# Seven block products for the gradient of w_down, interleaved with those of w_gate and w_up

## The chip, the cores and the metric

The kernel runs on one core of a Trainium2 chip. The metric is device time in microseconds (us) of one execution of the whole program; lower is better. "Before" is the kernel without the change, "after" the one with it.

## The reference

The program is the forward and backward pass of one transformer block in bf16: a pre-norm linear-attention layer, then a pre-norm SwiGLU feed-forward layer, with sequence length 2048, width D = 640 and hidden width F = 1728. It returns the block's output and the gradients of x, wqkv, wo, w_gate, w_up and w_down. What matters here is the feed-forward half, with n the normalised input of that layer:

```python
g = silu(n @ w_gate)          # n: 2048 x 640, w_gate and w_up: 640 x 1728
u = n @ w_up
out = (g * u) @ w_down        # w_down: 1728 x 640
# backward, with dy = grad_out (2048 x 640), m = g * u, dm = dy @ w_down.T:
# d_w_gate = n.T @ dg     (640 x 1728)
# d_w_up   = n.T @ du     (640 x 1728)
# d_w_down = m.T @ dy     (1728 x 640); the kernel forms its transpose, dy.T @ m (640 x 1728)
```

All three weight gradients are sums over the 2048 tokens, that is 16 token tiles of 128 rows.

## The kernel before, in words

**Groups.** The feed-forward backward pass runs in four groups of hidden columns, numbered 0 to 3, of width w = 448, 448, 448 and 384 (`GW`, `GO`). A group has two stages.

**Stage one, the SwiGLU loop.** For each pair of token tiles t, t+1 TensorE forms n @ w_gate (`pg`, L731) and n @ w_up (`pu`, L736), and in group 2 also dm (`pdm`, L417). ScalarE makes the sigmoids and bf16 copies (L752 to L758), and VectorE seven elementwise products and sums (L764), which leave m in the tile `m_s` [128, 16, 448] and the gradients dg and du side by side in `dd[0]` (token tiles 0 to 7) and `dd[1]` (tiles 8 to 15).

**Staging.** The next stage of the program needs dg and du transposed. So for each token tile SyncE's queue issues a transposing DMA of that tile's dg and du from `dd` into a small staging tile `stg` (L767), and then a store from there to the DRAM scratch `scr_dT` (L720). `stg` has three buffers, used in turn; a tile's transpose waits for the store of the tile three before it. GpSimd's queue stores `m_s` to `scr_m`, four token tiles at a time (L772).

**Stage two, the weight gradients** (`dw_group`; called "the gradient stage" below). TensorE forms the gradients of the group's columns. Rows of each 640-row gradient are five tiles of 128, i = 0 to 4. For d_w_gate and d_w_up, tiles 0 to 3 are formed by a Winograd form of Strassen's algorithm: the tokens are halved (k = 0, 1), the rows are halved (m = 0, 1, two tiles each, u = 0, 1), and the columns are the two halves dg | du of `dd`; seven block products (`prod`, L646, eight matmuls of w columns for each u) replace eight. VectorE makes the sums of operands: `S` and `S3` from n (`hn`), and `T1` to `T4` from `dd`, written over parts of `dd` and `m_s` (all L642). ScalarE copies partial results out of PSUM (L673, L685, L689, L698), VectorE adds them up into `dwev` tiles, and GpSimd's queue stores those (L652). Tile 4 of d_w_gate and d_w_up, and all five tiles of the transposed d_w_down, are plain accumulations over 16 token tiles by the helper `dw` (matmul L806, copy out of PSUM L808, store L810).

The orders of TensorE, VectorE and ScalarE in the gradient stage are the order in which the code is written (a manual schedule), and every engine works through its queue in order. PSUM is four buffers `mm` of two banks; `fpool` has six buffers for SwiGLU temporaries and results on their way out.

**Around it.** After a group's last staging store SyncE goes on with other loads and transposes (L258, L713, L190). In group 3 ScalarE's queue issues the load of the first transposed columns (`cols`, L157) ahead of its copies. After group 3 comes the input gradient (`ps_dhn`, L108).

Of the kernel before, what the change touches and what calls it, by code (L numbers as in the profile page):

```python
# [20 lines left out]
def kernel(  # L21
# [591 lines left out]
    zpad = wB.enter_context(tc.tile_pool(name="zpool", bufs=1)).tile([P, 4, 64], BF16, name="zpad")  # L613
    nc.gpsimd.memset(zpad[:], 0.0)

    with tc.manual_schedule(engines={EngineType.SP}):
# [10 lines left out]
        def dw_group(g, w, m_s, dd, dw, dwd_part, dgu_part):


# [14 lines left out]
            def prod(out, lhs, rhs, first):  # L644
                for t in range(8):
                    nc.tensor.matmul(out, lhsT=lhs[:, t, :], rhs=rhs[:, t, :], start=(first and t == 0),  # L646
                                     stop=(t == 7), skip_group_check=not first)

            def store(ev, n, m):
                for u in range(2):  # L650
                    i = 2 * m + u
                    nc.gpsimd.dma_start(out=(out_4, out_5)[n][i * P:(i + 1) * P, GO[g]:GO[g] + w], in_=ev[:, u, :w])  # L652

            U = range(2)
# [669 lines left out]
```

## Time and profile before

| | |
|---|---|
| median of 3 runs | 796.48 us (796.11 to 797.13) |
| profiled execution, first to last instruction | 794.5 us |
| matmul busy | 790.2 us, 99% of the span, 5315 matmuls |
| VectorE busy | 566.9 us, 71% |
| ScalarE busy | 288.1 us, 36% |
| GpSimd busy | 172.7 us, 22% |

Times in views of the trace are us from the start of the span. In the page and the views PE is TensorE's matmuls, PEld its weight loads, DVE VectorE, ACT ScalarE, POOL GpSimd and SP SyncE; "SPq" rows are instructions of SyncE that issue a DMA. L with a number is a line of the kernel. A row of the timeline has start, length, engine, line, operation, the tiles written and read, the shape, the count, and in brackets how long the engine had been idle before and what ended that. Matmuls overlap: the time of one row runs to the end of its last matmul, and the next row starts before that. The median lies 2.0 us above the span: what lies around the first and the last instruction.

### The profile page before, as it was taken

The page shows a single profiled execution, that of the slowest core. Times are in us where ns is not written, and L with a number is a line of the kernel's source. Part 1 is how long each engine was busy: PE and PEld are TensorE (multiplying, and loading weights), DVE is VectorE, ACT ScalarE, POOL GpSimd, SP SyncE. Part 2 cuts the span into 40 slices and gives each one's busy share as a digit, 9 for nine tenths or more (in the row PEclk, how much of TensorE's full clock was granted, in tenths as well). Part 3 has the DMA queues.
Part 4 walks back from the last instruction along what each step waited for, and adds up shares of the span by engine and source line. Part 5 has one row for each costly group of instructions (what it writes and reads, how often), then busy time and mean ns, then how long its engine had stood idle before and what let it go on. Part 6 is the DMA issues. An engine that isn't in the chain of part 4 may idle for free.

```text
span 794.5 us, 13629 instructions
## 1 busy us (share of the span) xinstructions
PE 790.2 (99%) x5315; PEld 506.5 (64%) x5315; DVE 566.9 (71%) x1015; ACT 288.1 (36%) x414; POOL 172.7 (22%) x305
## 2 busy tenths in 40 slices
PE   9999999999999999999999999999999999999998
PEld 7776566555555555555666777777777777777665
DVE  7989988894497648845975259998897366635773
ACT  6962532760283045402831123223313133324010
POOL 4600047411201110012042102111221121113230
PEclk9999999999999999999999999999999999999999
DMA  9799999999679877892798657976598959999992
GB/s 259 161 241 305 198 225 254 257 264 234 176 160 236 211 175 191 217 246 68 147 216 217 247 152 193 211 197 168 127 238 177 177 135 155 189 223 261 208 259 83
DMA packets 286705, 160.11 MB, mean 202 GB/s; under 512 B 241564, under 2 KB 275485, under 8 KB 286640
## 3 DMA queue, kind: packets, MB, share of 16 engines
q1 hardware_dynamic: 268912, 99.56, 61.7%
q0 software_dynamic: 14832, 54.36, 22.4%
q10 hardware_dynamic: 2896, 5.33, 2.0%
q8 instruction: 41, 0.67, 0.4%
q14 instruction: 24, 0.20, 0.1%
HBM read 47.68 MB, written 53.66 MB: 128 GB/s over the span
## 4 chain that ended last, share of the span: by engine, by line
PE 97%; DMA 1%; DVE 1%; POOL 0%; issue 0%; SPq 0%; DVEq 0%
PE ps_dhn L108 15%; PE ps_dw L806 10%; PE ps_dxn L1069 8%; PE pu L736 7%; PE ps_wa L646 7%; PE pg L731 7%; PE ps_dwqk L986 5%; PE ps_dm L417 5%; PE ps_kq L305 4%; PE ps_oa L1139 4%; PE ps_wc L646 3%; PE ps_gt L861 3%; PE ps_dp L108 3%; PE ps_dk L108 3%; PE ps_y L508 3%; PE ps_a L571 3%
## 5 line engine op out<-in xcount | busy, mean ns | idle before, releaser
L108 PE MATMUL ps_dhn<-wgT,cols 128*128 128x320 bf16 x864 | 119.5, 299 | 0.0
L108 PEld LDWEIGHTS <-cols 128*128 128x128 bf16 x864 | 84.5, 98 | 32.9
L146 DVE CUSTOM_DVE_ANT_0 lb_a<-lb_dy,hn 128x640 bf16<-128x640 bf16 x32 | 26.4, 825 | 59.0 <-ACT lb_dy L144 59.0
L736 PE MATMUL pu<-wgu,hnT 128*128 128x448 bf16 (+1 forms) x320 | 63.6, 346 | 0.0
L731 PE MATMUL pg<-wgu,hnT 128*128 128x448 bf16 (+1 forms) x320 | 63.6, 346 | 0.0
L806 PE MATMUL ps_dw<-m_s,dh 128*128 128x448 bf16 (+1 forms) x320 | 60.4, 346 | 0.0
L1069 PEld LDWEIGHTS <-ring 128*128 128x128 bf16 x480 | 47.0, 98 | 18.2
L1069 PE MATMUL ps_dxn<-wqkvT,ring 128*128 128x320 bf16 x320 | 51.3, 299 | 0.0
L736 PEld LDWEIGHTS <-hnT 128*128 128x128 bf16 x320 | 31.3, 98 | 27.1
L806 PEld LDWEIGHTS <-dh 128*128 128x128 bf16 x320 | 31.3, 98 | 27.1
L731 PEld LDWEIGHTS <-hnT 128*128 128x128 bf16 x320 | 31.3, 98 | 27.0
L417 PEld LDWEIGHTS <-dh2T 128*128 128x128 bf16 x320 | 31.0, 98 | 25.1
L417 PE MATMUL ps_dm<-wdT,dh2T 128*128 128x448 bf16 (+1 forms) x240 | 46.5, 344 | 0.0
L144 ACT ACTIVATE lb_dy<-ps_dhn,rstd 128x640 bf16<-128x640 f32 x16 | 12.7, 794 | 91.5 <-PE ps_dhn L108 91.5
L305 PE MATMUL ps_kq<-wqk,xnT 128*128 128x320 bf16 x320 | 44.9, 299 | 0.3 <-DMA wqk<-in_A_wqkv_dram 0.2
L752 ACT ACTIVATE dd<-pg 128x896 bf16<-128x896 f32 (+1 forms) x32 | 28.5, 891 | 40.4 <-PE pg L731 38.0
L642 DVE TENSOR_TENSOR dd<-dd 128x3584 bf16<-128x3584 bf16 (+1 forms) x12 | 23.1, 1954 | 22.8 <-PE ps_wa L646 15.6
L305 PEld LDWEIGHTS <-xnT 128*128 128x128 bf16 x320 | 30.9, 98 | 12.7 <-issue 0.5
L646 PEld LDWEIGHTS <-S 128*128 128x128 bf16 x256 | 25.1, 98 | 21.7
L772 POOL DMA_DIRECT2D scr_m<-m_s x16 | 12.1, 758 | 122.6 <-DVE m_s L764 122.6
L986 PEld LDWEIGHTS <-hn 128*128 128x128 bf16 x320 | 31.0, 98 | 12.0
L150 ACT ACTIVATE lb_a<-hn,lb_k 128x640 bf16<-128x640 bf16 x32 | 29.5, 920 | 21.8 <-DVE lb_k L149 18.8
(210 smaller groups left out, 1527.1 us busy)
## 6 DMA issues: line engine op xcount, KB each, us to landing
scr_dT<-stg SPq DMA_DIRECT2D x48, 224.0 KB, 2.6
cols<-scr_dT POOLq DMA_DIRECT2D x6, 1728.0 KB, 8.4
scr_m<-m_s POOLq DMA_DIRECT2D x12, 448.0 KB, 4.6
cols<-scr_dT ACTq DMA_DIRECT2D x2, 1728.0 KB, 10.5
scr_dT<-stg SPq DMA_DIRECT2D x16, 192.0 KB, 2.3
scr_pq<-pqa SPq DMA_DIRECT2D x4, 640.0 KB, 4.6
scr_xnT<-xnT SPq DMA_DIRECT2D x4, 640.0 KB, 5.3
scr_pk<-pk SPq DMA_DIRECT2D x4, 640.0 KB, 4.6
```

The lines of the kernel that those rows point to most:

```text
L108: nc.tensor.matmul(ps[:, ci, :320], lhsT=lhs(k), rhs=rhs(k, *NCH[ci]), start=(start and k == 0), stop=(stop and k == n - 1))
L150: nc.scalar.activation(out=a[:], in_=xhat, func=ACT.Identity, scale=k[:, 1:2], bias=k[:, 0:1])
L305: nc.tensor.matmul(ps[:, ci, :320], lhsT=xnT[:, t, k, :], rhs=wqk[:, k, w0 + n0:w0 + n1], start=(k == 0), stop=(k == DT - 1))
L417: nc.tensor.matmul(ps[:, c, :w], lhsT=dh2T[:, kt, (t + c) * P:(t + c + 1) * P], rhs=wdT[:, kt, o:o + w], start=(kt == 0), stop=(kt == DT - 1))
L646: nc.tensor.matmul(out, lhsT=lhs[:, t, :], rhs=rhs[:, t, :], start=(first and t == 0), stop=(t == 7), skip_group_check=not first)
L731: nc.tensor.matmul(pg[:, c, :w], lhsT=hnT[:, kt, (t + c) * P:(t + c + 1) * P], rhs=wg[:, kt, 0:w], start=(kt == 0), stop=(kt == DT - 1))
L736: nc.tensor.matmul(pu[:, c, :w], lhsT=hnT[:, kt, (t + c) * P:(t + c + 1) * P], rhs=wg[:, kt, w:2 * w], start=(kt == 0), stop=(kt == DT - 1))
L752: sig = nc.scalar.activation(out=dg, in_=pg[:, :, :w], func=ACT.Sigmoid)
L806: nc.tensor.matmul(ps[:, c, :w], lhsT=lhs(t), rhs=rhs(t), start=(t == 0), stop=(t == ST - 1))
L986: nc.tensor.matmul(ps[:, ci, :320], lhsT=xn_r[:, t, i * P:(i + 1) * P], rhs=dq[t // 8][:, t % 8, n0:n1] if which == 0 else dk[:, t, n0:n1] ...
L1069: nc.tensor.matmul(ps[:, ci, :320], lhsT=lhs[:, i, :], rhs=rhs[:, i, n0:n1], start=(k == 0 and i == 0), stop=(k == 2 and i == DT - 1))
L1139: nc.tensor.matmul(out, lhsT=lhs[:, k, :], rhs=rhs[:, k, :], start=(start and k == 0), stop=(stop and k == HK - 1), skip_group_check=not s ...
```

## The change

Tiles 0 to 3 of the transposed d_w_down are now formed by seven block products too: tokens halved, rows halved, and the group's w columns of `m_s` halved into h = w/2 (224, in group 3 192). Each product is eight matmuls of h columns for each u. So 64 matmuls of w columns are replaced by 112 of h columns in each group. Tile 4 stays a plain accumulation, and it now shares its PSUM tile `f1` with tile 4 of d_w_gate, as the first work of the stage; tile 4 of d_w_up moves into the middle.

The operand sums of the new products: `sd` (two tiles from `fpool`), made and then updated twice from `dh2` (dy), as `S` is from `hn`; `F1` to `F4`, written over quarters of `m_s`; and `sd3`, for which there was no free memory: it is written over the three staging buffers. To that end the staging buffers become one tile `stgs` [128, 3, 7, 128], which `stage()` hands out slot by slot; `sd3[0]` and `sd3[1]` lie in its first 2048 of 2688 columns, so each of them covers parts of two slots. `T4` moves from `m_s` into `dd[1]`, the kept partial results lie in quarters of `m_s`, `zpad` comes from `fpool`, and `fpool`'s buffers grow from 896 to 1024 elements.

```diff
+    stgs = const.tile([P, 3, 7, P], BF16, name="stgs")
+    stgn = [0]
     def stage():
-        return small.tile([P, 7, P], BF16, name="stg", tag="stg", bufs=3)
+        stgn[0] += 1
+        return stgs[:, stgn[0] % 3]
...
+            T1, T2, T3, T4 = B11, B11, B12, B21
+            E11, E12 = m_s[:, 0:8, 0:h], m_s[:, 0:8, h:w]
+            E21, E22 = m_s[:, 8:16, 0:h], m_s[:, 8:16, h:w]
+            F1, F2, F3, F4 = E11, E11, E12, E21
...
+            sd = [ff("Sd").rearrange("p (t c) -> p t c", t=8) for _ in U]
+            sd3 = [stgs.rearrange("p a k c -> p (a k c)")[:, u * 8 * P:(u + 1) * 8 * P].rearrange("p (t c) -> p t c", t=8)
+                   for u in U]
...
-            dw([dwd_part(0), dwd_part(1)], nc.vector.tensor_copy, first=True)
+            for u in U:
+                tt(sd[u], dh_(1, 0, u), dh_(1, 1, u), ALU.add)
             for u in U:
-                tt(S[u][:], hn_blk(1, 0, u), hn_blk(1, 1, u), ALU.add)
...
+                lhs, rhs, _ = (dwd_part(4), dgu_part(4, 0))[c]
+                nc.tensor.matmul(f1[:, c, :w], lhsT=lhs(t), rhs=rhs(t), start=(t == 0), stop=(t == ST - 1))
...
+            q(0, lambda u: dh_(0, 0, u), E11, True)
+            q(1, lambda u: dh_(0, 1, u), E21, True)
...
+            tt(F1, E12, E11)
+            s1d = fp("s1d")
+            copy(out=s1d, in_=both(0))
+            evd0 = fw("dwd0")
+            tt(quarter(evd0, 0), both(1), s1d, ALU.add)
+            tt(F3, E22, E12)
+            for u in U:
+                tt(S3[u][:], hn_(0, 0, u), hn_(1, 0, u))
             tt(T1, B12, B11)
...
             store(ev, 0, 0)
-            dw([dwd_part(4)], nc.vector.tensor_copy)
+            q(1, lambda u: sd[u], F1, True)
+            for u in U:
+                tt(sd3[u], dh_(0, 0, u), dh_(1, 0, u))
+            pc = mm("ps_wc")
+            for u in U:
+                tt(sd[u], sd[u], dh_(0, 0, u))
+            tt(F2, E22, F1)
             for u in U:
                 prod(pc[:, u, :w], S[u], T1, True)
-                tt(S[u][:], S[u][:], hn_blk(0, 0, u))
+            q(0, lambda u: sd[u], F2, False)
+            u2d = fp("u2d")
+            copy(out=u2d, in_=both(0))
+            tt(F4, E21, F2)
+            for u in U:
+                tt(S[u][:], S[u][:], hn_(0, 0, u))
             tt(T2, B22, T1)
+            lhs, rhs, dst = dgu_part(4, 1)
...
+            q(0, lambda u: sd3[u], F3, False)
...
-            dw([dwd_part(2), dwd_part(3)], nc.vector.tensor_copy)
```

`q` is two `prod` of h columns, into one bank of the PSUM tile `qd`; `both` reads that bank.

VectorE, group 0's gradient stage, before: from the sums of n to T2. In these rows `S_2244` and `S_2245` are S3, `dd<-dd` is T1, then T2 and T3, and `s_2361` and `s_2364` are the partial results s1; a name in brackets behind "waits" is a semaphore (DMAHW of SyncE's and ScalarE's DMAs, DMASW of GpSimd's).

```order
L642 TENSOR_TENSOR S_2244<-hn 128x1024
L642 TENSOR_TENSOR S_2245<-hn 128x1024
L642 TENSOR_TENSOR dd<-dd 128x8x448 [waits DMAHW2_49,DMAHW4_49,DMAHW1_49,DMAHW6_49,DMAHW0_49,PE_49]
L642 TENSOR_TENSOR dwev<-ps_wa,s_2361 128x448 [waits Activation_49]
L642 TENSOR_TENSOR dwev<-ps_wa,s_2364 128x448 [waits Activation_49]
L808 CAST dwev<-ps_dw 128x448 [waits DVE_49,PE_49]
L642 TENSOR_TENSOR S<-S,hn 128x1024 [waits DVE_49,PE_49] x2
L642 TENSOR_TENSOR dd<-dd 128x8x448 [waits DVE_49]
```

The same place after: `dd<-dd` is T1, the two rows `stgs<-dh_1883` are sd3, `Sd<-Sd,dh_1883` is the first update of sd, and the two rows `m_s<-m_s` are F2 and F4.

```order
L644 TENSOR_TENSOR S_2227<-hn 128x1024
L644 TENSOR_TENSOR dd<-dd 128x8x448 [waits DMAHW2_49,DMAHW4_49,DMAHW1_49,DMAHW6_49,DMAHW0_49,PE_49]
L644 TENSOR_TENSOR dwev<-ps_wa,s_2346 128x448 [waits DMASW1_49,DMASW0_49,Activation_49]
L644 TENSOR_TENSOR dwev<-ps_wa,s_2349 128x448 [waits Activation_49]
L644 TENSOR_TENSOR stgs<-dh_1883 128x1024 [waits DMAHW2_49,DMAHW6_49,DMAHW1_49,DMAHW0_49]
L644 TENSOR_TENSOR stgs<-dh_1883 128x1024 [waits DMAHW7_49,DMAHW4_49]
L644 TENSOR_TENSOR Sd<-Sd,dh_1883 128x1024 [waits PE_49] x2
L644 TENSOR_TENSOR m_s<-m_s 128x8x224
L644 TENSOR_TENSOR m_s<-m_s 128x8x224 [waits DMASW7_49,DMASW6_49,DVE_49]
```

The two sums into `stgs` stand ahead of the update of sd, of F2, and so of everything that VectorE does later in the stage, and they wait for DMAs: the semaphore counts are those of the transposes into the slots that they write over and of the stores out of them. The three slots hold token tiles 13, 14 and 15 by then. In groups 0, 2 and 3 the first sum's count includes the store of tile 15, the group's last; in group 1 the second sum's does.

TensorE, group 0, at the end of the product S by T1 (`ps_wc`): before, tile 2 of d_w_down follows.

```order
L646 MATMUL ps_wc<-dd,S 128x448
L646 LDWEIGHTS S
L646 MATMUL ps_wc<-dd,S 128x448
L806 LDWEIGHTS dh_1887
L806 MATMUL ps_dw<-m_s,dh_1887 128x448
```

After, the product sd by F2 follows there (`ps_qd`).

```order
L648 MATMUL ps_wc<-dd,S 128x448
L648 LDWEIGHTS S
L648 MATMUL ps_wc<-dd,S 128x448
L648 LDWEIGHTS Sd
L648 MATMUL ps_qd<-m_s,Sd 128x224
```

What stood there before read `dh2` and `m_s` as they were; what stands there now needs the updated sd and F2, and so waits for VectorE.

VectorE at the end of group 0's SwiGLU loop, before and then after; `dd<-a,nsg` is the last gradient dg, of token tiles 14 and 15.

```order
L764 TENSOR_TENSOR m_s<-m_s,u 128x896 [waits DVE_49,Activation_49]
L764 TENSOR_TENSOR a<-u,dm_842 128x896
L764 TENSOR_TENSOR dd<-a,nsg 128x2x448 [waits DVE_49]
L808 CAST dwev<-ps_dw 128x896 [waits PE_49]
L642 TENSOR_TENSOR S<-hn 128x1024 [waits DMASW6_49,DMASW5_49,DMASW7_49,DMASW3_49,DMASW1_49]
```

In the rows of after, `Sd<-dh_1883` is the first making of sd.

```order
L860 TENSOR_TENSOR m_s<-m_s,u 128x896 [waits DVE_49,Activation_49]
L860 TENSOR_TENSOR a<-u,dm_843 128x896
L644 TENSOR_TENSOR Sd<-dh_1883 128x1024 [waits DMASW2_49,DMASW3_49,DMASW1_49,DMASW0_49]
L860 TENSOR_TENSOR dd<-a,nsg 128x2x448 [waits DVE_49]
L644 TENSOR_TENSOR Sd<-dh_1883 128x1024
```

One of the two sums into sd has slipped ahead of the last gradient, in groups 0, 1 and 3; in group 2 both stand behind it. SyncE's queue has the same instructions in the same order before and after.

More of the change, by code (lines that the diff above doesn't have):

```diff
@@ L635, in dw_group @@
             B11, B12 = dd[0][:, :, 0:w], dd[0][:, :, w:2 * w]
             B21, B22 = dd[1][:, :, 0:w], dd[1][:, :, w:2 * w]
-            T1, T2, T3, T4 = B11, B11, B12, m_s[:, 0:8, :w]
-            kept = m_s[:, 8:16, :].rearrange("p t n -> p (t n)").bitcast(FP32).rearrange("p (k u n) -> p k u n", k=2, u=2)
-            u2, u3 = kept[:, 0, :, :w], kept[:, 1, :, :w]
-            def tt(out, in0, in1, op=ALU.subtract):
-                nc.vector.tensor_tensor(out=out, in0=in0, in1=in1, op=op)
[L644 to L654, printed above, removed]
+            T1, T2, T3, T4 = B11, B11, B12, B21
+            E11, E12 = m_s[:, 0:8, 0:h], m_s[:, 0:8, h:w]
+            E21, E22 = m_s[:, 8:16, 0:h], m_s[:, 8:16, h:w]
+            F1, F2, F3, F4 = E11, E11, E12, E21
+            kept = m_s.rearrange("p t n -> p (t n)").bitcast(FP32).rearrange("p (t n) -> p t n", t=ST)
@@ new lines, in dw_group @@
+            u2d = fp("u2d")
+            copy(out=u2d, in_=both(0))
+            tt(F4, E21, F2)
+            for u in U:
+                tt(S[u][:], S[u][:], hn_(0, 0, u))
+            tt(T2, B22, T1)
+            lhs, rhs, dst = dgu_part(4, 1)
+            for t in range(ST):
+                nc.tensor.matmul(pa[0][:, 1, :w], lhsT=lhs(t), rhs=rhs(t), start=(t == 0), stop=(t == ST - 1))
+            ev = fw("dwev")
+            copy(out=ev[:, 0, :w], in_=pa[0][:, 1, :w])
+            nc.gpsimd.dma_start(out=dst[:, GO[g]:GO[g] + w], in_=ev[:, 0, :w])
@@ L691, in dw_group @@
+            copy(out=quarter(evd1, 0), in_=both(0))
+            store_d(evd1, 1)
             ev = fw("dwev")
-            tt(ev[:, :, :w], pc[:, :, :w], u3, ALU.add)
+            for u in U:
+                tt(four(ev[:, u, :w]), four(pc[:, u, :w]), u3(u), ALU.add)
             store(ev, 1, 1)
-            late = m_s[:, 12:16, :].rearrange("p (k u) n -> p k u n", k=2)
-            ev = late[:, 0]
+            ev = fw("dwev")
             for u in U:
-                prod(pa[u][:, 0, :w], hn_blk(1, 1, u), T4, False)
+                prod(pa[u][:, 0, :w], hn_(1, 1, u), T4, False)
@@ L931, in load_pk @@
         def load_pk(t):
-            pkrs[t] = small.tile([P, D], BF16, name="pkr", tag="stg", bufs=3, padded_shape=[P, 7 * P])
-            pool_store(pkrs[t][:], scr_pk_v[:, t, :])
+            pkrs[t] = stage()[:, 0:DT, :].rearrange("p k c -> p (k c)")
+            pool_store(pkrs[t], scr_pk_v[:, t, :])
         load_pk(0)
@@ L1036 @@
                 pkr = pkrs.pop(t)
-                nc.vector.tensor_scalar(out=pkr[:], in0=pkr[:], scalar1=-1e-6, scalar2=1.0, op0=ALU.add, op1=ALU.min)
+                nc.vector.tensor_scalar(out=pkr, in0=pkr, scalar1=-1e-6, scalar2=1.0, op0=ALU.add, op1=ALU.min)
                 tk = wk("tk", pool=1)
```

108 lines of the change are left out of this document (74 added, 34 removed).

## The prediction

> **What bounds the kernel now.** I read the page first, then the chain that ended last, then the timeline of TensorE in the gradient stages.
>
> ```profile
> PE 790.2 (99%) x5315; PEld 506.5 (64%) x5315; DVE 566.9 (71%) x1015; ACT 288.1 (36%) x414; POOL 172.7 (22%) x305
> PE 97%; DMA 1%; DVE 1%; POOL 0%; issue 0%; SPq 0%; DVEq 0%
> 172.05 12.11 PE ps_dw L806 x64
> 400.83 10.40 PE ps_dw L806 x64
> 467.93 7.33 PE ps_dhn L108 x54
> ```
>
> TensorE is 97% of the chain. The chain's rows give its pace: 64 matmuls of 448 columns in 12.11 us are 189.2 ns each, 64 of 384 in 10.40 are 162.5, 54 of 320 in 7.33 are 135.8. That is a line of 0.417 ns per column plus 2.3 ns.
>
> The gradient stage of group 0 begins at the first row below and ends where the next group's loop begins; the later rows are the starts in groups 1, 2 and 3 and the end of group 3.
>
> ```profile
> 171.88 6.22 PE L806 MATMUL ps_dw<-m_s,dh 128*128 128x448 bf16 x32
> 214.26 2.05 PE L731 MATMUL pg<-wgu,hnT 128*128 128x448 bf16 x10
> 244.52 6.22 PE L806 MATMUL ps_dw<-m_s,dh 128*128 128x448 bf16 x32
> 332.30 6.22 PE L806 MATMUL ps_dw<-m_s,dh 128*128 128x448 bf16 x32
> 400.67 5.36 PE L806 MATMUL ps_dw<-m_s,dh 128*128 128x384 bf16 x32
> 437.07 3.15 PE L108 MATMUL ps_dhn<-wgT,cols 128*128 128x320 bf16 x22
> ```
>
> Group 0 takes 42.38 us, which is 224 x 189.2 ns: TensorE waits for nothing. Group 3 takes 36.4 us, 224 x 162.5 ns. So fewer columns are worth their full time, and any wait put into this stage costs its full time. Below, "+x" means x us after the start of a group's stage.
>
> **TensorE's own part.** In each group 64 matmuls of w columns go and 112 of w/2 come. By the line, 224 columns take 95.7 ns and 192 take 82.4. Groups 0 to 2: 12.11 - 112 x 0.0957 = 1.39 us saved each; group 3: 10.40 - 112 x 0.0824 = 1.17. In all 5.3 us, if nothing waits. A doubt is whether weight loads keep up with so short a matmul:
>
> ```profile
> L534 PEld LDWEIGHTS <-wvo x30: 95/98/98, 81.1 to 82.7; 128*128 128x128 bf16 x30
> L534 PE MATMUL ps_kvt<-yk,wvo x30: 179/216/216, 81.3 to 82.7; 128*128 128x120 bf16 x25, 128*128 128x40 bf16 x5
> ```
>
> Thirty loads of 98 ns each, one for every matmul of 120 or 40 columns, start within 1.6 us: about 55 ns apart. Loads overlap one another, and 95.7 ns leaves room. The Trainium skill, "TensorE: Matmul & The Clock Gate", section "LDWEIGHTS (loading the stationary operand)", puts a load at its column count over 1.2, 107 ns for 128; were that the pace, 112 x 107 ns would be 12.0 us and the saving nearly nothing. The rows above say otherwise, and I take 5.3.
>
> **The wait that the change adds.** The two sums sd3 are written into the staging slots. They cannot start before the transposes into those slots and the stores out of them are done, that of token tile 15 among them. Queued behind them on VectorE are the update of sd and F2, for which TensorE waits at the product sd by F2, and then T2, T3, T4, F4 and every add of results. So the question is when the staging ends. In group 0 it is far behind:
>
> ```profile
> 150.43 12.08 SPq L767 DMA_TRANSPOSE stg<-dd  x2
> 185.02 1.22 SPq L767 DMA_TRANSPOSE stg<-dd  x1
> 188.82 2.02 DVE L642 TENSOR_TENSOR dd<-dd 128x3584 bf16<-128x3584 bf16 x1 [7.19 <-DMA stg<-dd]
> 203.18 1.28 SPq L767 DMA_TRANSPOSE stg<-dd  x1
> 204.51 4.79 SPq L720 DMA_DIRECT2D scr_dT<-stg  x2
> L720 SPq DMA_DIRECT2D scr_dT<-stg x1: 320/320/320, 209.0 to 209.0; - x1
> DMA to landing us min/median/max: 2.1/2.1/2.1
> q1 hardware_dynamic: 15901, 6.86, 74.0%
> q0 software_dynamic: 688, 1.95, 18.3%
> ```
>
> The first transposes of group 0 start at 150.43. That of tile 7 starts at 185.02 and ends at 188.8, where VectorE, which needs it for T1, had sat idle 7.19 us: a compute engine's own record of the lag. Tile 15 is issued at 203.18, and its store, alone in the sixth row, starts at 209.0 and lands 2.1 us later, at 211.1 or +39.2. The last two rows (the DMA view from 172 to 212) show why: SyncE's and GpSimd's queues fill 92% of the 16 engines. All that lies ahead of the stage is the same after the change.
>
> The other groups, each with SyncE's last two stores and their landing:
>
> ```profile
> L720 SPq DMA_DIRECT2D scr_dT<-stg x2: 320/322/325, 263.2 to 264.9; - x2
> DMA to landing us min/median/max: 2.2/2.4/2.5
> L720 SPq DMA_DIRECT2D scr_dT<-stg x2: 320/322/324, 343.6 to 345.5; - x2
> DMA to landing us min/median/max: 2.0/2.2/2.4
> L720 SPq DMA_DIRECT2D scr_dT<-stg x2: 320/518/715, 429.3 to 432.0; - x2
> DMA to landing us min/median/max: 1.8/2.4/3.0
> 412.39 0.40 ACTq L157 DMA_DIRECT2D cols<-scr_dT  x1
> 417.59 0.33 SPq L720 DMA_DIRECT2D scr_dT<-stg  x1
> 424.17 1.22 SPq L767 DMA_TRANSPOSE stg<-dd  x1
> ```
>
> They land at +22.8 in group 1, +15.6 in group 2 and +33.7 in group 3, where the load of `cols` at 412.39 holds SyncE's queue from 417.59 to 424.17.
>
> When does VectorE come to sd3? TensorE's order is f1 (32 matmuls of w), four products of h (32), four of w (32), sd by F1 (16 of h), S by T1 (16 of w), sd by F2. In group 2 that is 6.05 + 3.07 + 6.05 + 1.53 + 3.03 = +19.7 for sd by F2. T1 follows the first half of the w products, +12.5 with a matmul's 0.35 us to its end; with 1.95 for T1, and the second add of s1 after +15.5, VectorE is at sd3 at about +16.1. Durations are from these rows:
>
> ```profile
> 179.15 2.48 DVE L642 TENSOR_TENSOR S<-hn 128x1024 bf16<-128x1024 bf16 x4
> 196.91 3.95 DVE L642 TENSOR_TENSOR dd<-dd 128x3584 bf16<-128x3584 bf16 x2
> ```
>
> A sum of 1024 elements takes 0.60 us, one of 3584 1.95, so F2 with 1792 takes 1.0, with 1536 (group 3) 0.87. From the landing to the product sd by F2 lie two sd3 (1.2; in group 1 only the second waits for tile 15, 0.6), two sd (1.2), F2 and 0.1 for a semaphore: 3.5, 2.9 and, in group 3, 3.4. Behind it TensorE has 64 matmuls of h and 80 of w: 6.1 + 15.1 = 21.3 us, in group 3 18.3. VectorE keeps ahead in that rest: F4, two S and T2 end 4.2 us after F2, where TensorE wants T2 at 6.1; T3 and T4 have more room.
>
> The landings may come earlier, since VectorE's stop holds back GpSimd's stores of results. By group 0's landing five stores of 112 KB fewer are out; at 1.95 MB in 18.3% of 40 us that is at most 2.1 us of DMA time. Between 0 and 2.1 I take 1.0 in groups 0 and 3, 0.4 in group 1.
>
> - Group 0: 38.2 + 3.5 + 21.3 = 63.0 for 42.4: **+20.6**.
> - Group 1: 22.4 + 2.9 + 21.3 = 46.6 for 42.4: **+4.2**.
> - Group 2: the slots are free 0.5 us before VectorE wants them, and F2 is ready at +19.5, 0.2 before its use: **-1.4**.
> - Group 3: 32.7 + 3.4 + 18.3 = 54.4 for 36.4: **+18.0**.
>
> **The clock after a wait.** TensorE would stand still some 20 us in group 0, 5 in group 1 and 16 in group 3. Before, it never stands still, so the nearest row is the first of the program:
>
> ```profile
> 1.11 3.60 PE L341 MATMUL ps_warm<-ones 128*128 128x128 bf16 x32 [1.11 <-DVE ones L244]
> ```
>
> These 32 take 106 ns each, against 55.7 by the line: half speed for at least 3.6 us, 1.8 us lost. Whether a wait in mid-program brings that back, no row here shows: 0 to 1.8 each. I take 1.8 in groups 0 and 3, half in group 1: **+4.5**. The Trainium skill, same page, section "The HAM clock gate (the "warmup" mystery)", says that one idle window of about 3.4 us halves the clock and that a like stretch of work restores it.
>
> **What hides the rest.** VectorE gets per group eight sums of 1024 (4.8 us) and four F (4.0) more, and loses three copies; they lie beside TensorE's 41 us. The sum into sd that slipped ahead of the last gradient moves that by 0.5 us; the row it delays, and those of groups 1 and 3:
>
> ```profile
> 176.86 0.62 DVE L764 TENSOR_TENSOR dd<-a,nsg 128x896 bf16<-128x896 bf16 x1
> 249.45 0.62 DVE L764 TENSOR_TENSOR dd<-a,nsg 128x896 bf16<-128x896 bf16 x1
> 405.61 0.56 DVE L764 TENSOR_TENSOR dd<-a,nsg 128x768 bf16<-128x768 bf16 x1
> ```
>
> The gradient would end at 178.0, 250.6 and 406.7, and f1's 31st matmul wants it at 177.6, 250.2 and 405.5. So TensorE waits 0.4, 0.4 and 1.1 us there. These waits, and one for T1 in group 0 (188.8 as before), are swallowed, since the landing sets what follows; without it they cost 1.9. GpSimd's memset of zpad, ahead of one `scr_m` store in group 3, and the first transposes of a group, which now also wait for a product long done, delay nobody.
>
> **Sum:** 20.6 + 4.2 - 1.4 + 18.0 + 4.5 = +45.9. On the span, 794.5 + 45.9 = 840.4; the median of the runs lies 2.0 above the span, so 842.4.
>
> **Rivals.**
>
> 1. *The staging is out in time* and VectorE never waits at sd3. It decides if the last store lands before about +16 in every group. Then the saving stays, less the waits at f1: 796.5 - 5.3 + 1.9 = 793.1. For it: group 2 is so already. Against: in group 0 nine transposes are still to be issued at +13. Chance 0.04.
> 2. *Staging runs much faster once GpSimd's stores stop*, by 6 us in groups 0 and 3: 842.4 - 10 = 832, with the 1.0 taken already. Against: from tile 7 to tile 15 the transposes start 2.3 us apart, and issuing one alone takes 1.2 to 1.3 of that. Chance 0.10.
> 3. *The clock is not lost:* 842.4 - 4.5 = 837.9. Chance 0.14.
> 4. *More waits behind F2*, where VectorE and ScalarE catch up, of 2 us in each of the three groups, and none of the DMA relief (2.4): 850.8. Chance 0.12.
>
> My forecast, 842.4, has 0.60. The range goes from 830, a little below rival 2, to 852, above rival 4; it leaves out rival 1 and what is worse than both bounds. A measurement of this kernel can tell 0.2%, 1.6 us, from no change. Faster by more than that: 0.03; within it: 0.01, a rival 1 with a little more waiting; slower: 0.96.
>
> **What would show it.** In the profile of after, the rows of `stgs<-dh` on VectorE should name a DMA as releaser with some 18 us of idle in group 0, 5 in group 1, 14 in group 3 and none in group 2; TensorE should name VectorE at the product sd by F2, and its busy share should fall from 99% to about 94%. Matmuls of 224 columns should run 96 ns apart. Matmuls twice as long just behind a wait would show the clock. The prediction is wrong if VectorE passes `stgs<-dh` at once in group 0, or if the last `scr_dT` store lands before 190.

## The result, and the profile after

The changed kernel takes **848.95 us** (median of 4 runs, 844.84 to 857.3) against 796.47 (4 runs, 796.11 to 797.13): a ratio of 1.0657, 95% interval 1.062 to 1.0695. The forecast was 842.4, with a range of 830 to 852. The profile is of the fastest of the four runs: 844.84, span 843.1.

The page, engines and the chain that ended last:

```profile
PE 795.3 (94%) x5507; PEld 526.7 (62%) x5507; DVE 598.6 (71%) x1071; ACT 297.5 (35%) x434; POOL 172.4 (20%) x305
PE 67%; DVE 12%; issue 9%; DMA 7%; SPq 2%; ACT 2%; POOL 1%; DVEq 0%; ACTq 0%; POOLq 0%
```

TensorE is busy 94% of a longer span, and the chain has left it: a third of the chain is VectorE (12%), issuing (9%), DMAs (7%) and the smaller ones. What TensorE waits for (total, times, longest):

```profile
PE ps_qd L648 <- DVE m_s L644: 38.0, 4, 17.9
PE ps_dwv L127 <- DMA mats<-scr_Yt: 2.8, 2, 2.6
PE ps_dw L699 <- DVE dd L860: 1.6, 3, 1.0
PE ps_qd L648 <- DVE dwd L644: 0.8, 1, 0.8
```

The first line is the product sd by F2, the third f1. The timeline of TensorE, with the start of each group's stage (`ps_dw<-m_s,dh`), sd by F2, what follows it, and the start of the input gradient:

```profile
171.30 2.81 PE L699 MATMUL ps_dw<-m_s,dh 128*128 128x448 bf16 x14
210.05 3.15 PE L648 MATMUL ps_qd<-m_s,Sd 128*128 128x224 bf16 x16 [17.88 <-DVE m_s L644]
212.99 4.56 PE L760 MATMUL ps_wa<-dd,hn 128*128 128x448 bf16 x16
217.38 1.70 PE L648 MATMUL ps_qd<-m_s,stgs 128*128 128x224 bf16 x16
264.69 2.81 PE L699 MATMUL ps_dw<-m_s,dh 128*128 128x448 bf16 x14
289.72 3.15 PE L648 MATMUL ps_qd<-m_s,Sd 128*128 128x224 bf16 x16 [4.71 <-DVE m_s L644]
359.62 2.81 PE L699 MATMUL ps_dw<-m_s,dh 128*128 128x448 bf16 x14
380.47 1.69 PE L648 MATMUL ps_qd<-m_s,Sd 128*128 128x224 bf16 x16 [0.95 <-DVE m_s L644]
427.80 2.44 PE L699 MATMUL ps_dw<-m_s,dh 128*128 128x384 bf16 x14
460.56 2.72 PE L648 MATMUL ps_qd<-m_s,Sd 128*128 128x192 bf16 x16 [14.48 <-DVE m_s L644]
479.64 0.98 PE L108 MATMUL ps_dhn<-wgT,cols 128*128 128x320 bf16 x6
481.76 18.50 PE L108 MATMUL ps_dhn<-wgT,cols 128*128 128x320 bf16 x135
```

And the sums sd3 on VectorE, one row or two for each group:

```profile
206.50 1.29 DVE L644 TENSOR_TENSOR stgs<-dh 128x1024 bf16<-128x1024 bf16 x2 [16.50 <-DMA scr_dT<-stgs]
285.42 0.69 DVE L644 TENSOR_TENSOR stgs<-dh 128x1024 bf16<-128x1024 bf16 x1 [3.75 <-DMA scr_dT<-stgs]
286.77 0.69 DVE L644 TENSOR_TENSOR stgs<-dh 128x1024 bf16<-128x1024 bf16 x1 [0.65 <-DMA scr_dT<-stgs]
376.91 1.29 DVE L644 TENSOR_TENSOR stgs<-dh 128x1024 bf16<-128x1024 bf16 x2 [0.74 <-DMA scr_dT<-stgs]
457.14 1.29 DVE L644 TENSOR_TENSOR stgs<-dh 128x1024 bf16<-128x1024 bf16 x2 [7.72 <-DMA scr_dT<-stgs]
```

VectorE stands at sd3 behind the staging's stores, and TensorE stands behind VectorE. Behind the wait TensorE also runs slower for a while: its granted clock, 1.00 in this stage of before, is 0.50 from 210 to 215.

**Where the time went.** The starts of the groups cut the span into stretches, and each is compared with the same stretch of before. Group 0 is 264.69 - 171.30 = 93.39, before 72.64: +20.75 (the SwiGLU loop of the next group is in it, which did not change). Six `ps_dhn` matmuls slipped ahead of the end of group 3, so its end is put at 481.76 - 6 x 0.136 = 480.95, and "rest" is what follows. The table has every profiled kernel cut in this way, in us more than before. The changed kernel's stretches sum to 48.6, the difference of the spans.

| kernel | median us | ratio [95%] | up to group 0 | group 0 | 1 | 2 | 3 | rest |
|---|---|---|---|---|---|---|---|---|
| the changed kernel | 848.95 | 1.0657 [1.062, 1.0695] | -0.6 | +20.8 | +7.2 | -0.2 | +16.8 | +4.7 |
| e2_wait | 830.51 | 1.0418 [1.0374, 1.0461] | +0.3 | +18.9 | +1.1 | 0.0 | +15.6 | +0.1 |
| e1_elsewhere | 812.70 | 1.0208 [1.0162, 1.0254] | +0.2 | +3.7 | -0.6 | -1.0 | +11.1 | +3.3 |
| e6_only0 | 828.81 | 1.0396 [1.0317, 1.0476] | +0.6 | +22.8 | -0.2 | -1.0 | +10.0 | +5.5 |
| e3_warm | 846.28 | 1.0616 [1.0543, 1.0688] | -0.2 | +19.8 | +9.9 | -0.5 | +16.8 | 0.0 |
| e11_after_cols | 839.93 | 1.0550 [1.0524, 1.0577] | -0.2 | +18.5 | +10.1 | -0.4 | +12.6 | +8.0 |
| e4_late | 825.71 | 1.0352 [1.0332, 1.0373] | +0.8 | +4.3 | +4.0 | +3.8 | +11.7 | +3.9 |
| e5_late_f1 | 826.63 | 1.0394 [1.0357, 1.0430] | +0.5 | +6.5 | +3.9 | +3.8 | +13.6 | +1.3 |
| e7_zpad | 808.68 | 1.0152 [1.0118, 1.0186] | -0.3 | +3.8 | -0.6 | -0.8 | +10.3 | +0.4 |
| e8_cols | 803.96 | 1.0077 [1.0051, 1.0103] | +0.2 | +6.1 | -0.5 | -1.0 | +5.5 | +0.1 |
| e9_all | 804.66 | 1.0086 [1.0060, 1.0112] | +0.2 | +9.4 | -0.2 | -0.2 | +1.9 | +0.7 |
| e10_best | 803.52 | 1.0082 [1.0062, 1.0103] | -0.5 | +0.7 | +0.3 | +0.3 | +2.7 | +5.0 |
| e12_tidy | 796.93 | 0.9992 [0.9968, 1.0017] | +0.1 | -1.4 | -0.9 | -0.9 | +0.3 | +5.4 |

Each ratio is taken against runs of before on the same chip, whose medians lie between 796.46 and 797.05. One execution of e4_late and one of e12_tidy fell in a slower state of the chip; they count in the medians and not in the ratios.

### The profile page after: what moved, and what is told of

Its sections match the earlier page's. It is cut to its first block, busy times and chain, and to the rows that moved or that the text cites. A ratio compares the mean times of both kernels' runs of the same rounds, so it can differ in the third digit from the quotient of the medians.

```text
span 843.1 us, 14105 instructions
## 1 busy us (share of the span) xinstructions
PE 795.3 (94%) x5507; PEld 526.7 (62%) x5507; DVE 598.6 (71%) x1071; ACT 297.5 (35%) x434; POOL 172.4 (20%) x305
## 4 chain that ended last, share of the span: by engine, by line
PE 67%; DVE 12%; issue 9%; DMA 7%; SPq 2%; ACT 2%; POOL 1%; DVEq 0%; ACTq 0%; POOLq 0%
PE ps_dhn L108 14%; PE ps_dxn L1151 8%; PE ps_kq L312 5%; PE ps_dwqk L1068 5%; PE ps_dm L424 5%; PE ps_wa L648 3%; DMA scr_dT<-stgs 3%; DVE dd L860 3%; DVE m_s L860 3%; DVE nsg L860 3%; PE ps_gt L943 3%; PE ps_dp L108 3%; PE ps_y L515 3%; PE ps_dk L108 3%; PE ps_a L578 3%
## 5 line engine op out<-in xcount | busy, mean ns | idle before, releaser
L648 PE MATMUL ps_qd<-m_s,Sd 128*128 128x224 bf16 (+1 forms) x192 | 23.8, 287 | 38.8 <-DVE m_s L644 38.0
L648 PEld LDWEIGHTS <-Sd 128*128 128x128 bf16 x192 | 20.4, 109 | 43.0 <-DVE Sd L644 33.7
L424 PEld LDWEIGHTS <-dh2T 128*128 128x128 bf16 x320 | 31.0, 98 | 25.1
L868 POOL DMA_DIRECT2D scr_m<-m_s x16 | 12.1, 756 | 120.5 <-DVE m_s L860 120.5
L648 PE MATMUL ps_wa<-dd,hn 128*128 128x448 bf16 (+1 forms) x192 | 36.4, 346 | 0.0
## 6 DMA issues: line engine op xcount, KB each, us to landing
cols<-scr_dT ACTq DMA_DIRECT2D x2, 1728.0 KB, 10.1
```

The source lines that it names most:

```text
L424: nc.tensor.matmul(ps[:, c, :w], lhsT=dh2T[:, kt, (t + c) * P:(t + c + 1) * P], rhs=wdT[:, kt, o:o + w], start=(kt == 0), stop=(kt == DT - 1))
```

## The experiments

The theory: the loss is VectorE's wait at sd3 for the staging, together with the clock that TensorE loses behind its own wait. The rivals: that the seven products themselves, or other waits that they bring, cost the time.

**e2_wait: the wait without the products.** Before, with the staging tile `stgs` of the change and, behind the adds of s1, two sums into its slots; nothing reads them.

```diff
             store(ev, 0, 0)
+            for u in U:
+                tt(stgs.rearrange("p a k c -> p (a k c)")[:, u * 8 * P:(u + 1) * 8 * P].rearrange("p (t c) -> p t c", t=8),
+                   dh2[:, 0:8, u * P:(u + 1) * P], dh2[:, 0:8, (u + 2) * P:(u + 3) * P])
             dw([dwd_part(4)], nc.vector.tensor_copy)
```

> As before, with one tile for the three staging slots and, behind the first stored result of each gradient stage, two sums from dy written over them as sd3 is; nothing reads them. So the wait alone, without the products. Theory: VectorE stops at the two sums until the last store has landed, about +36 to +39 in group 0 and +30 to +34 in group 3; behind them stands the copy of tile 4 of d_w_down out of PSUM, whose buffer TensorE wants at +24.2 and +20.8. Waits of 13 to 17 and 10 to 15 us, none in groups 1 and 2, and 5 for the clock: 825 to 833. Rival (the products themselves): two sums more cost nothing, 796 to 798.

Measured: 830.51, 34 us above before. TensorE's rows behind the two long waits:

```profile
212.68 8.82 PE L813 MATMUL ps_dw<-m_s,dh 128*128 128x448 bf16 x32 [16.07 <-DVE dwev L815]
454.41 8.26 PE L813 MATMUL ps_dw<-m_s,dh 128*128 128x384 bf16 x32 [12.54 <-DVE dwev L815]
```

No new product is in this kernel, and two sums for each group bring most of the loss: VectorE copies results out of PSUM too late, and TensorE waits for that. Groups 1 and 2 lose little, as their staging is nearly out. The same two sums stand in groups 1 and 2 as well, so it is not their own time that costs. The wait alone is sufficient for a loss of 34 us.

**e1_elsewhere: the products without the wait.** The changed kernel with sd3 written over S3; part of the w_up gradient is then not formed.

```diff
-            sd3 = [stgs.rearrange("p a k c -> p (a k c)")[:, u * 8 * P:(u + 1) * 8 * P].rearrange("p (t c) -> p t c", t=8)
-                   for u in U]
...
+            sd3 = [S3[u][:] for u in U]
```

> As after, but sd3 is written over the tiles of S3, not over the staging slots; the number and the order of the instructions stay. The products S3 by T3 then read the wrong sum, so part of the gradient of w_up is left wrong. Theory (VectorE's wait for the staging carries the loss): no wait at sd3; the product sd by F2 starts at most 1 us late in each group; time 796.5 - 5.3 (fewer columns) + 1.9 (waits at f1), and up to 1 more for small waits at F2: 793 to 795. Rival (the loss comes from the seven products themselves: VectorE's added sums, short matmuls, a slower clock): at least half of the 48 us stays, 820 or more.

Measured: 812.70. That is 36 us less than the changed kernel, so the wait at sd3 is also necessary for most of the loss. But it is not 793 to 795. Of the 16.7 us that the profiled span is above that of before, 11.1 lie in group 3. There TensorE, and ahead of it ScalarE, show:

```profile
429.45 2.72 PE L648 MATMUL ps_qd<-m_s,Sd 128*128 128x192 bf16 x16 [7.64 <-DVE m_s L644]
412.52 0.80 ACT L700 CAST dwev<-ps_dw 128x768 bf16<-128x768 f32 x1 [8.06 <-PE ps_qd L648]
421.09 0.48 ACT L738 COPY s<-ps_wa 128x384 f32<-128x384 f32 x1 [7.39 <-DMA scr_dwdT<-zpad]
425.05 0.48 ACT L738 COPY s<-ps_wa 128x384 f32<-128x384 f32 x1 [3.49 <-DMA out_dram<-dwev]
```

With the first wait gone a second stands at the same product. Two of `fpool`'s six buffers are held by sd for the whole stage, and one was given to zpad. So the copies of s1 (the last two rows) take buffers whose last contents (zpad, then f1's results) GpSimd's queue is still storing. ScalarE waits for the DMAs, VectorE for ScalarE at the adds of s1, and F2 stands behind those. The copy of f1 (the second row) is late too: the view names TensorE, but just ahead of that copy, at 412.05, ScalarE's queue issues the load of cols. The theory was incomplete, and e7 and e8 take this up.

**e6_only0: the wait in group 0 alone.** e1_elsewhere, with sd3 over the staging slots in group 0 only.

```diff
             sd3 = [stgs.rearrange("p a k c -> p (a k c)")[:, u * 8 * P:(u + 1) * 8 * P].rearrange("p (t c) -> p t c", t=8)
+                   if g == 0 else S3[u][:] for u in U]
```

> As e1, but group 0 keeps sd3 in the staging slots. Theory, with each group's loss its own: e1 plus 20.75 us that group 0's period grew in after and 1 that it shrinks in e1: about 815. If the waits move from group to group instead (staging that falls behind once stays behind): groups 1 and 3 would show waits at F2 here too, which e1's do not.

Measured: 828.81 (823.95 and 833.67), that is 16 us above e1_elsewhere and 14 above the 815 expected, since what e1_elsewhere still loses is in it too: the same 21.75 on top of 812.7 would be 834.5. In its profile group 0 is +22.8, near the changed kernel's +20.8, and the other groups are within 1.2 us of e1_elsewhere. So the groups' losses add up, to some 6 us.

**e3_warm: TensorE kept busy while it waits.** The changed kernel with matmuls that serve nothing ahead of sd by F2.

```diff
+            for _ in range((84, 14, 0, 82)[g]):
+                nc.tensor.matmul(pa[0][:, 1, :w], lhsT=dh2[:, 0, 0:P], rhs=dd[0][:, 0, w:2 * w], start=True, stop=True)
             q(0, lambda u: sd[u], F2, False)
```

> As after, with matmuls whose result is overwritten, put ahead of the product sd by F2: 84 in group 0, 14 in group 1, 82 in group 3, 15.9, 2.6 and 13.3 us of work, while TensorE waits anyway. Theory (a clock that falls while TensorE stands still): the 16 matmuls behind the wait take 1.5 us from first to last start and not 2.9, and the next 16 take 3.0 and not 4.4; 7 us less than after in all, if the waits are as long as in after's profile. Rival (these matmuls are slow because VectorE works through its queue beside them at that moment): they stay slow, and the time stays.

Measured: 846.28 (841.99 and 850.57), 2.7 less than the changed kernel, within the spread of both. Of the time as a whole it decides nothing: in groups 0 and 1 the filler ended 2.85 and 3.93 us too early, and those waits again cost the clock. In group 3 it fitted:

```profile
210.81 3.11 PE L648 MATMUL ps_qd<-m_s,Sd 128*128 128x224 bf16 x16 [2.85 <-DVE m_s L644]
464.55 1.48 PE L648 MATMUL ps_qd<-m_s,Sd 128*128 128x192 bf16 x16 [0.54 <-DVE m_s L644]
```

The 16 matmuls in the second row take 1.48 us, those of the changed kernel 2.72 behind its 14.48 us, with the same sums on VectorE beside them; the granted clock just behind is 1.00 here and 0.50 there. So the slow matmuls come from TensorE's standing still, not from their form or place, nor from VectorE's work.

**e11_after_cols: the load of cols behind the staging.** The changed kernel with one line moved to another queue.

```diff
-                load_cols(0, act_load)
+                load_cols(0, sync_load)
```

Here `sync_load` issues on SyncE, behind the last `store_dT`.

> The changed kernel with one edit: the first load of cols is issued by SyncE behind the last staging store instead of by ScalarE ahead of its copies. In the changed kernel a store of group 3's staging is issued at 442.81 and the next transpose only at 448.52, behind that load. If the staging of group 3 is held by the load: sd3 starts 5 to 7 us earlier, TensorE's wait there falls from 14.5 to 8 or 9, and the whole by 5.5 to 7.5, to 841 to 843. If the load only shares the DMA engines' time (rival), the staging ends when it did, and the time stays within 2 us of 849.

Measured: 839.93, 9 us below the changed kernel. SyncE's queue at the place where the load held it, in the changed kernel:

```profile
442.81 0.33 SPq L816 DMA_DIRECT2D scr_dT<-stgs  x1
448.52 1.22 SPq L863 DMA_TRANSPOSE stgs<-dd  x1
```

and in e11_after_cols:

```profile
443.91 0.33 SPq L819 DMA_DIRECT2D scr_dT<-stgs  x1
444.85 1.22 SPq L866 DMA_TRANSPOSE stgs<-dd  x1
```

The hold of 5.7 us is gone, sd3 starts at +25.1 instead of +29.3, and group 3 loses 4.1 us less. That is less than the 5.5 to 7.5 expected: of the hold 0.9 us are left, and the transpose ahead of it goes out 1 us later in the stage in this run. The 9 us between the medians are more than this edit can show in group 3. The two profiled executions, here the slowest of four and for the changed kernel the fastest, have the same span of 843.1, with 2.9 us more in group 1 and 3.3 more in the rest. So the direction is shown, the size only as 4.

**e4_late and e5_late_f1: sd3 at the end of the stage.** If the wait is all, the products should pay once sd3 stands where the staging is surely out. e4_late moves sd3 and its product last, which takes two more partial results (`v2d`, `x4d`) in `fpool`:

```diff
+            v2d = fp("v2d")
+            tt(v2d, both(1), u2d, ALU.add)
             tt(F4, E21, F2)
...
+            for u in U:
+                tt(sd3[u], dh_(0, 0, u), dh_(1, 0, u))
...
+            q(0, lambda u: sd3[u], F3, True)
```

> As after, but with sd3 and its product at the end of the stage: VectorE makes sd3 ahead of the last two adds, TensorE takes sd3 by F3 as its last product, and two more adds on VectorE put the results together. All results as in the reference. Theory: the slots are free by +35 to +38 in group 0 and +29 to +33 in group 3, and the last product is wanted at about +39.9 and +35, so no wait is left but those at f1 (1.9): 796.5 - 5.3 + 1.9, about 793, and a spread between runs as small as that of before. Rival (staging goes on holding up the stage, or the scheme's other waits eat the saving): 797 or more.

e5_late_f1 also puts f1's last two matmuls behind the first four new products:

```diff
+            f1_mm(steps[:-2])
...
             q(1, lambda u: dh_(0, 1, u), E21, True)
+            f1_mm(steps[-2:])
```

> As e4, with f1's last two matmuls, those that read the last gradient, put behind the first four products of d_w_down. Theory: the waits at f1 of 0.3, 0.25 and 1.0 us in after's profile go, so 1.5 to 2 us below e4: about 791.5. Rival (something else is late there in their place, F1 or the copies of f1): as e4, or above it.

Measured: 825.71 and 826.63. Both miss, by 33 and 35 us: no wait at sd3 is left, but each of groups 0 to 2 is still about 4 us above before (6.5 in group 0 of e5_late_f1), and group 3 11.7 and 13.6, with a wait of 4 to 5 us at sd by F2 as in e1_elsewhere. TensorE in groups 0 and 1, and VectorE ahead of the first row, in e4_late:

```profile
200.01 4.88 PE L648 MATMUL ps_wa<-dd,S 128*128 128x448 bf16 x16 [2.39 <-DVE dd L644]
276.94 3.20 PE L648 MATMUL ps_wa<-dd,S 128*128 128x448 bf16 x16 [2.39 <-DVE dd L644]
```

```profile
195.19 0.63 DVE L644 TENSOR_TENSOR v2d<-ps_qd,u2d 128x448 f32<-128x448 f32 x1 [3.27 <-ACT u2d L751]
197.93 2.02 DVE L644 TENSOR_TENSOR dd<-dd 128x3584 bf16<-128x3584 bf16 x1
```

T2 (the last row) came 2.39 us late in each of groups 0 to 2, because my new add v2d, which waits for ScalarE, and F4 stood ahead of it. The order of VectorE has no slack to spare there. f1's wait was gone in e5_late_f1, and the time was no better: in group 0 a wait of 3.30 us stood in another place.

**e7_zpad and e8_cols: the second wait in group 3.** e7_zpad is e1_elsewhere with zpad in a tile of its own, and s1 for u = 0 in the buffer of s1d:

```diff
-                s1 = ff("s1").bitcast(FP32)[:, :w]
+                s1 = ff("s1").bitcast(FP32)[:, :w] if u else s1d.rearrange("p u n -> p (u n)")
```

e8_cols is e7_zpad with the load of cols on SyncE, as in e11_after_cols.

> e1_elsewhere with two temporaries placed elsewhere: the zero padding in a small tile of its own, and the first partial result s1 in the buffer of s1d, which is dead by then (so the second s1 takes the old buffer that the first one had, and no copy of s1 waits for a store). As in e1_elsewhere a part of the w_up gradient is left wrong. In e1_elsewhere TensorE still lost 7.64 us at sd by F2 in group 3; ScalarE stood 7.39 us at its first copy of s1 behind the store of the zero padding, and 3.49 at the second behind the store of f1's results. Theory A (the buffers of fpool, held by GpSimd's stores): VectorE gets through T1 at about 419.0, two adds (1.1), sd3 (1.2), sd (1.2) and F2 (0.9), so F2 comes at 423.4 where TensorE wants it at 421.7; the wait falls from 7.64 to about 1.7, with the slow clock behind it: 812.7 - 5.9 - 2.1 = 804 to 806. Theory B (ScalarE held by the load of cols in front of its copies): nothing changes by more than 1 us, 811 to 814.

> e7_zpad with the first load of cols issued by SyncE behind the last staging store, instead of by ScalarE ahead of its copies. In e1_elsewhere ScalarE idled until 412.05, 2.5 us after f1 was ready, and the transposes stood from 420.4 to 425.0 behind that load. Theory A and B together: f1's copy, s1d, F3 and T1 come 2.5 us sooner, F2 is ready before TensorE wants it, the remaining 1.7 goes: 801 to 804. If B is nothing: as e7_zpad within 0.5 us. Against: the load of 1.77 MB now starts some 10 us later, at about 422, and lands 9 us on at 431, close to its first use at 436; if it is late, the input gradient waits for it and the time is up to 5 us above e7_zpad.

Measured: 808.68 and 803.96. e7_zpad missed. TensorE's wait in group 3 stayed 7.31. Of the 3.8 us between the profiled spans of e1_elsewhere and e7_zpad 2.8 lie in the rest, which the edit does not touch, and 0.8 in group 3. ScalarE's second copy of s1, and the DMA view from 408 to 432 (KB each, median us from issue to landing):

```profile
424.02 0.48 ACT L740 COPY s<-ps_wa 128x384 f32<-128x384 f32 x1 [7.62 <-DMA out_dram<-dwev]
```

```profile
cols<-scr_dT ACTq DMA_DIRECT2D x1, 1728.0 KB, 11.7
out_dram<-dwev POOLq DMA_DIRECT2D x3, 96.0 KB, 6.3
```

So zpad was not what held F2: it was the buffer of f1's results, whose store took 9.5 us to land (issued at 414.38) beside the load of cols. e8_cols shows that most of it was the load: with it out of the way f1's copy comes at +6.6 instead of +9.9, its store lands after 5.3 us, the same copy of s1 comes at +16.4 instead of +21.2, TensorE's wait falls from 7.31 to 2.08, and group 3 from +10.3 to +5.5.

**e9_all, e10_best, e12_tidy: taking the waits away.** All three leave nothing out. e9_all joins e5_late_f1 and e8_cols, with T2 ahead of v2d and F4.

> All seven products with nothing left out, and each wait found so far taken away: sd3 and its product last in the group (as e4_late), f1's last two matmuls behind four of the new products (as e5_late_f1), the zero padding and s1 out of the way and cols on SyncE (as e8_cols), and on VectorE the update of S and T2 ahead of the add v2d and F4, with the product by F4 moved behind S3 by T3. In e4_late T2 came 2.39 us late in each of groups 0 to 2; in the new order it ends at about 196.4 where TensorE wants it at 197.5. If the change's cost is these waits and nothing else, the saving of 5.3 us appears, less what the tail lost (2 to 3 us, waits for scr_Yt and what lies around): 792 to 796. If the cost is that VectorE and ScalarE have too much to do beside TensorE (rival), new waits of 1 to 3 us each appear in every group, as in e4_late and e5_late_f1: 805 to 815.

Measured: 804.66. Group 3 fell to +1.9, but group 0 did not. Its T1 and T4 on VectorE:

```profile
190.57 2.02 DVE L649 TENSOR_TENSOR dd<-dd 128x3584 bf16<-128x3584 bf16 x1 [6.20 <-DMA stgs<-dd]
209.14 2.02 DVE L649 TENSOR_TENSOR dd<-dd 128x3584 bf16<-128x3584 bf16 x1 [4.19 <-DMA stgs<-dd]
```

The second row is a wait that the change itself brought, hidden behind sd3 in the changed kernel: T4 moved from `m_s` into `dd[1]`, over data that the transposes up to tile 15 must have read. e10_best writes T4 over `m_s`, puts tile 4 of d_w_up ahead of sd by F2 and of S by T1, and in groups 0 and 3 makes T1 behind F2; u3 goes into `dd[0]`:

```diff
-            T1, T2, T3, T4 = B11, B11, B12, B21
+            T1, T2, T3, T4 = B11, B11, B12, m_s[:, 8:16, :w]
```

> e9_all in another order, nothing left out. Left in e9_all were, in group 0, T1 behind the transpose of tile 7 (TensorE 3.84 us) and T4 behind that of tile 15 (VectorE 4.19, TensorE 2.42), each with the slow clock behind it, and 0.6 at S by T2 in every group. Here tile 4 of d_w_up goes in front of sd by F2, so that in groups 0 and 3 T1 has 4.5 us more; T4 is written over m_s instead of dd[1], and waits for no transpose; S by T2 comes two short products later. If the change's cost is its waits alone: group 0 from +9.4 to +1 or less, groups 1 and 2 from -0.2 to -1.2, group 3 from +2.7 to +1, the whole 794 to 798, level with before. Rival (the work beside TensorE is too much for VectorE and ScalarE, so a wait that is taken away comes back in another place): 801 to 806, as e9_all.

Measured: 803.52, while group 0 fell from +9.4 to +0.7. The rest is 5.0 longer. TensorE's waits in group 0 that come again in every group:

```profile
198.00 1.69 PE L653 MATMUL ps_qd<-m_s,Sd 128*128 128x224 bf16 x16 [0.62 <-ACT x4d L785]
204.85 1.67 PE L653 MATMUL ps_wa<-dd,S 128*128 128x448 bf16 x8 [0.62 <-ACT dd L798]
```

Each is a product right behind a copy that reads another part of the same PSUM tile, or writes another part of the same operand tile. e12_tidy moves those copies, and three adds that TensorE waited behind:

```diff
+            q(1, lambda u: sd[u], E22, False)
             x4d = fp("x4d")
             copy(out=x4d, in_=both(0))
-            q(1, lambda u: sd[u], E22, False)
...
-                return dd[0][:, 2 * u:2 * u + 2, 0:w].bitcast(FP32)
+                return S3[u].rearrange("p t c -> p (t c)").bitcast(FP32)[:, :w]
```

> e10_best with its remaining waits of TensorE taken away, nothing left out. In each group TensorE stood 0.62 us behind the copy x4d (the copy now comes behind the product sd by E22) and 0.62 behind the copy of u3 into dd[0] (u3 now goes into S3's own buffer), and 0.3 behind an add (both adds now behind both products); in group 3 F2 was 1.36 us late behind the second add of s1, which now follows F2. If those waits are what is left: 1.2 us less in each group and 1.5 more in group 3. Groups 0 to 2 then gain, from +0.7, +0.3 and +0.3 to -0.5, -0.9 and -0.9, group 3 goes from +2.7 to about 0; what follows group 3 was 5.0 us longer in e10_best and 0 to 0.7 in e7_zpad to e9_all, with nothing in the edits to explain it. Together 793 to 799, level with before or a little faster. Rival (taken-away waits return elsewhere): 801 to 805, as e10_best.

Measured: 796.93 against 796.73, ratio 0.9992 [0.9968, 1.0017]: level with before. The timeline of TensorE:

```profile
171.93 2.81 PE L706 MATMUL ps_dw<-m_s,dh 128*128 128x448 bf16 x14
243.19 2.81 PE L706 MATMUL ps_dw<-m_s,dh 128*128 128x448 bf16 x14
330.11 2.81 PE L706 MATMUL ps_dw<-m_s,dh 128*128 128x448 bf16 x14
397.57 2.44 PE L706 MATMUL ps_dw<-m_s,dh 128*128 128x384 bf16 x14
434.23 29.50 PE L108 MATMUL ps_dhn<-wgT,cols 128*128 128x320 bf16 x216
758.68 0.23 PE L127 MATMUL ps_dwv<-stgs,mats 128*128 128x120 bf16 x1 [2.24 <-DMA mats<-scr_Yt]
```

Group 0 takes 71.26 for 72.64, 1.38 less, and the input gradient starts 2.84 us earlier than before (434.23 for 437.07). The last row, 324 us on, gives it back: in this execution TensorE waits there for the transposes of `scr_Yt`, 2.6 us with the matmul behind it, and runs slower afterwards, which with a wait of 0.7 us elsewhere makes most of the +5.4 in the rest. The other executions have no profile, so that they differ in this manner is not shown, but their clocks go with it. Six of the eleven that the comparison uses have a mean clock of 1.000 and take 792.56 to 796.24; the five at 0.996 to 0.998 take 797.61 to 802.04. Before has such an execution too: one of its 17 on this chip, at 0.997, takes 802.67.

## Why the prediction came out as it did

**The wait at sd3: right in kind, place and sign.** e2_wait and e1_elsewhere show it from both sides. VectorE idles 16.5, 4.4 (3.75 + 0.65), 0.7 and 7.7 us at `stgs<-dh`, forecast 18, 5, none and 14. In group 3 VectorE had already stood 2.9 and 2.4 us at the adds of s1, the wait of e1_elsewhere, so less was left for sd3. TensorE waits 17.9, 4.7, 1.0 and 14.5 us, with some 20, 5, none and 16 forecast.

**The terms of the sum**, each stage with its clock, against the table:

- Group 0: 20.6 + 1.8 forecast, 20.75 measured. sd3 starts at +35.2, not +38.2: the last store goes out at about 204.0 (the second of the two stores issued from 202.33), not 209.0. The relief that I put between 0 and 2.1 and took as 1.0 was too small, or this run's DMAs were quicker. The second is at least part of it: T1, which waits for tile 7's transpose before VectorE stops, starts at +15.6 for +16.9 in before. And sd3 starts at +33.2, +35.5, +37.2 and +38.6 in e11_after_cols, e3_warm, e6_only0 and e2_wait, whose staging is the same. So the point that this term hangs on moves by 5 us from run to run, and the profile of before, with +39.2, lay at its late end.
- Group 1: 4.2 + 0.9 forecast, 7.15 measured. Of the difference 1.3 are the slow clock, 0.8 a wait behind F2.
- Group 2: -1.4 forecast, -0.2 measured. The slots came free 0.74 us after VectorE was there, not 0.5 before, and TensorE waited 0.95.
- Group 3: 18.0 + 1.8 forecast, 16.75 measured, with sd3 at +29.3 instead of +32.7.
- Everything behind group 3: 0 forecast, +4.7 measured; a term that the sum did not have.

That the sum came so close is in part luck. In the profile it is 2.7 us short (48.6 for 45.9), while its parts are off by -1.7, +2.1, +1.2, -3.1 and +4.7, and by -0.6 ahead of group 0. And the median lies 4.1 us above the profiled execution, which no term of the sum accounts for.

**The clock: right in kind, too small.** Behind the wait in group 0 the 16 matmuls of 224 columns and the 16 of 448 take 217.38 - 210.05 = 7.33 us, against 1.53 + 3.03 at the full pace: 2.8 us lost, and in the same way 2.2 and 2.1 in groups 1 and 3. That is 7.1 for my 4.5. I had taken 1.8 from the program's first 3.6 us. Rival 3 (no clock lost) falls.

**TensorE's own part, 5.3 us if nothing waits: the pace is shown, the whole sum is not.** Behind the slow stretch 16 matmuls of 224 columns take 1.53 us start to start, 95.7 ns each, as the line had it. And where no wait is left, in group 0 of e12_tidy, the stage is 1.38 us shorter, for 1.39 worked out. Groups 1 and 2 gain 0.9 each there, with a wait of 0.3 to 0.4 us left, and group 3 nothing, with 0.9 us of waits, so no kernel reached the 5.3. The Trainium skill, "TensorE: Matmul & The Clock Gate", section "LDWEIGHTS (loading the stationary operand)", puts a load of 128 columns at 107 ns; if that were the spacing, nearly nothing would be saved, and the 95.7 ns here do not bear it out.

**The waits at f1:** 0.4, 0.4 and 1.1 forecast, 0.30, 0.25 and 1.00 measured.

**The step that failed without showing in the result** is rival 1's price, 793.1 with the staging out in time, and behind it "VectorE keeps ahead in that rest" and "T3 and T4 have more room". With sd3 out of the way the time is 812.7, not 793.1. For what stands behind sd3 I had looked for waits only among engines. I had not asked who holds `fpool`'s buffers, with two of six taken by sd, nor what T4's new place in `dd[1]` must wait for. Rival 2 (staging runs 6 us faster) is half seen: 3 us. Rival 4's time, 850.8, is the nearest to the median, but its mechanism is not: behind F2 TensorE waited 0.8 us in all, while the staging was no slower but faster.

**What stays open.** The rest of the program is up to 8 us longer in some profiles and as before in others (the last column). Each of the profiles with +2 or more has TensorE waiting 1.9 to 3.9 us at `ps_dwv` for `scr_Yt`'s transposes, on SyncE's queue. In the changed kernel the order of that queue is the same as before, and neither the staging nor the seven products touch these transposes. The last two of them, in before and then in e12_tidy:

```profile
751.03 3.19 SPq L938 DMA_TRANSPOSE mats<-scr_Yt  x2
DMA to landing us min/median/max: 4.3/4.7/5.0
```

```profile
753.01 2.70 SPq L1038 DMA_TRANSPOSE mats<-scr_Yt  x2
DMA to landing us min/median/max: 4.8/5.2/5.6
```

In before the second is issued at 752.9 and lands at 757.2, and TensorE comes at 758.0: only 0.8 us behind it. In e12_tidy it is issued at 754.4 and lands at 759.2, and TensorE comes at 756.1. So part of the wait is the saving itself: with before's landing TensorE would still have stood there about 1.2 us (an estimate from these rows). What makes the landing a few microseconds later in one run than in another was not tried.

The four runs of the changed kernel lie 12 us apart, those of before beside them 1 us (7 us among the 17 on e12_tidy's chip). That its time hangs on the pace of DMAs goes with the 5 us by which the start of sd3 moves; that this is the whole of it is not shown.

## What to carry to other kernels

Memory that looks free because its owner is an engine's small temporary may belong to a DMA queue that lags by some 30 us; before an engine writes there, look up when the last transfer out of it lands, and what is queued on that engine behind the write. When a wait is to be removed, look for the next one at the same instruction: here it took five edits (staging, buffers, a load's traffic, an overwritten operand, copies beside products in one tile) before a saving could be seen, 1.4 us in one group and 0.9 in two. In a kernel whose bounding engine never waits, 5 us of its work saved are worth less than the one wait of 18 us that came with them, so the first question about a change is who waits for whom, not how many instructions it saves.
